# A searched instruction order for an attention and two feed-forward layers: new priorities and an explicit table

## The chip, the cores and the metric

The kernel runs on one core of a Trainium2 chip. The metric is the device time of one execution in microseconds (us). The core has five instruction queues: TensorE (PE, matrix products; PEld is its weight load), VectorE (DVE), ScalarE (ACT), GpSimd (POOL) and SyncE (SP, which issues the DMAs). Each queue runs its instructions strictly in the order of the program, and they wait for one another by semaphores. So the order in which a planner emits the work is the whole schedule.

## The reference

Three stages follow one another: causal attention with a learned decay (4 batches, 8 heads, 576 positions, head size 64), a feed-forward layer 512 → 2048 → 512 with PReLU, and a second one with Mish. Both feed-forward layers see 2304 tokens.

```python
scores = scale * np.matmul(q, k.transpose(0, 1, 3, 2))
cum = np.cumsum(np.log(np.clip(f, 0.0001, 1.0)), axis=-1)
scores = np.where(causal, -1e9, scores + cum[:, :, :, None] - cum[:, :, None, :])
attn = np.exp(scores - np.max(scores, axis=-1, keepdims=True))
attn = attn / (np.sum(attn, axis=-1, keepdims=True) + 1e-09)
x = np.matmul(attn, v)            # then heads side by side: 2304 x 512
h = x @ w_in; g = np.maximum(h, 0.0) + alpha * np.minimum(h, 0.0); x = g @ w_out
h = x @ w_in2; g = h * np.tanh(np.log1p(np.exp(h))); out = g @ w_out2
```

The weights come as 64-bit floats and are turned into 32-bit ones on the core.

## The kernel before

**Stages.** Attention works on 16 pairs of heads. For each pair there are twelve score products that serve only the row maximum (L616, written to one of three PSUM banks b4, b5, b6). VectorE reduces each of them (L623) and so frees its bank. Five small transposes (L635) bring the maxima into rows; then come the scores themselves (L660, banks b0 to b3 in twos), the exponential (L670 on ScalarE), the sums (L708) and the product with v (L742, banks b4 to b6 again). X holds the result, 512 x 2304.

Each feed-forward product is done in three passes: both operands are split into a high part in the reduced 32-bit format and a low part, the rest (L321 casts the high part, L331 subtracts for the low one). For the activations these are xh and xl, for the hidden layer g, for the weights w. L786 to L788 are the first product (three passes, four chunks of 512, 384 tokens to a block, six blocks); below, three such passes are a unit. L851 to L853 are the second product of layer 1, L862 to L864 that of layer 2. In layer 1, four of the sixteen slices of the hidden layer are done first for each block (`group_a`, products on bank b7 during the attention and on b4 to b7 after it; L323 or L321 copies their result out), for three blocks while the attention still runs. The other twelve follow in `moe_block`. Weights arrive as 64-bit words and are converted by L399 (ACT) and L401, L403, L405 (DVE); those of layer 2 are converted during layer 1, stored, and fetched back.

At the start GpSimd and VectorE fill constant tiles (L527 to L553). One of them is the unit matrix `ident` (masks.py:197 and 199). TensorE then runs 30 products of it with itself (L519, "warm", 60 instructions in the trace), and four more behind each of the first pair's products. The decay goes f → clamp (L532) → logarithm (L533, ACT) → running sum (L534) → high part (L537, ACT) and low part (L538), and from there by DMA (L579) into three rows of KM, an operand of L616.

**What sets the order.** Every operation is added to `Plan` with its engine, a cost in us, a wanted time `at` and the things it reads and writes. `PRIO` (by stage name and number in the stage) shifts the wanted time; `ENG` picks the engine where two or three could do the operation. `schedule` is a list scheduler: the engine that is free first takes the ready operation with the smallest priority, with `HOP` for a handover between engines and a rule that GpSimd and some VectorE work exclude each other (`door`). `emit` runs it ten times, forward and backward by turns, keeps the order with the smallest estimate, and calls the operations in that order. PSUM banks of the shared groups are taken from that best schedule (`self.taken`).

Of the kernel before, what the change touches and what calls it, by code (L numbers as in the profile page):

```python
# [16 lines left out]

PRIO = {'': {0: -17.5, 1: -17.2, 2: -11, 3: -11.5, 4: -11.4}, 'A0': {0: -1.0, 1: -1, 2: 7.5, 3: -8.5}, 'A0g': {1: -13.5, 2: -16.5, 3: -21.1}, 'A1': {0: 50, 1: -24.7, 2: 1, 3: -42.4}, 'A1g': {0: -16.6, 1: 5, 2: 6, 3: -0.2}, 'A2': {0: 48.5, 2: -4, 3: 15.2}, 'A2g': {0: 12, 1: -22.0, 2: 30.6, 3: 15}, 'A3': {0: 9.5, 1: -8, 2: -42.3, 3: -28.5}, 'A3g': {0: 31, 1: 4, 2: 54.2, 3: -6}, 'AX': {1: 10.1, 2: 21.5, 3: -5, 4: 12, 5: 11.5, 6: 25.1, 7: 21}, 'B0': {0: 1.3, 1: -1.3, 2: 2, 3: 8, 4: -1}, 'B1': {0: 0.5, 2: -26.9, 3: 2, 4: -17.3}, 'B2': {0: 4.5, 1: 0.5, 2: -31.4, 3: 7.5, 4: 8.5}, 'B3': {0: -15.7, 1: 24, 2: -57.2, 3: 7, 4: 1.5, 5: -3.5, 6: 1.4, 7: 2.5}, 'H0': {0: -1, 1: -0.5, 2: -2.5, 3: -33, 4: 9, 5: 16.5, 6: 11.5, 7: 10}, 'H1': {0: -45.2, 1: -4.5, 2: -40.5, 3: -36.5, 4: -2.5, 5: 4.5, 6: 1, 7: 8, 8: -70.4, 9: -7.1, 10: 3.7, 11: -4, 12: -33.6, 13: -5.5, 14: -30.5}, 'LB2': {0: -1.6, 1: 2, 2: 2, 3: 2}, 'LQ2': {0: -38.9, 1: 20}, 'LV2': {0: 6.3, 1: 20}, 'M2': {0: 20, 1: 6.1, 2: 20, 3: 27.7, 4: 20, 5: 20, 6: 20, 7: -2.4, 8: 20, 9: 21.2, 10: 16.0, 11: 47.1, 12: 20, 13: 30.5, 14: 20, 15: 20, 16: 20, 17: 20, 18: 20, 19: 30.1, 20: 20, 21: 20.5, 22: 20, 23: 20.6}, 'NM2': {0: 0.6, 2: 4.6}, 'O0': {0: -1, 1: -8.5, 2: -11.1, 3: -37, 4: 29.1, 5: 2.5, 6: -0.5, 7: -0.1}, 'O1': {0: -8.5, 1: 22.5, 2: 17.4, 3: 41.2, 4: -9.7, 5: 25, 6: 15.8, 7: 36.5, 8: 62.5}, 'R2': {6: -0.3, 7: -4.9, 9: -1.8, 10: 3.8, 11: -25.5}, 'ST0': {1: 3.2, 3: -4.8}, 'ST1': {0: -6.4, 2: -1.6}, 'ST2': {2: -17.2}, 'ST3': {3: 53.3}, 'T2': {0: -5, 1: -5, 2: -5, 3: -5}, 'W': {0: 36.6, 1: -4, 2: -12.5, 3: -7.6, 4: 34, 5: -33.3, 6: -58.3, 7: 9.5, 8: 30, 9: -6.5, 10: -29.8, 11: -5, 12: 1, 13: -25.9}, 'WA': {0: 2, 1: 4.0, 3: -24.8, 4: -10.5, 5: 6.5, 6: 2, 7: 5, 8: -41.5, 9: -12.9, 10: -6.3, 11: 10.8, 12: 7.5}, 'WF': {0: 33.9, 1: 5.4, 2: -47.5}, 'WS': {0: 1, 1: 4.2, 2: -17, 3: -56, 4: -2, 5: -12.8, 6: -1.4, 7: -6.7, 8: -15.5, 9: -26, 10: -6.8, 11: -40.8, 13: -5.5}, 'X0': {0: -1.6, 1: -52.2, 2: 38.0, 3: -5, 4: -2, 5: 11.5, 6: 22.0, 7: -19.1}, 'X1': {0: -10.8, 1: -14.4, 2: -13.2, 3: -22, 4: -4.5, 5: 16.4, 6: -22.5, 7: -49.3}, 'alph': {0: 60.6, 1: 32.4}, 'const': {0: 46.5, 1: 2}, 'pro2': {1: -42.3, 3: -16.0, 7: -1.2, 8: -7.9, 11: 10.3, 12: 7.7, 13: 19.7, 18: -5.1, 21: -1.9, 22: 17.9, 24: -4.5, 25: 15.7, 26: -9.5, 27: 35.1}, 'warm2': {0: 6.0}}  # L20
ENG = {('A0g', 0): 'ACT', ('A0g', 2): 'ACT', ('A0g', 3): 'POOL', ('A1g', 0): 'ACT', ('A2g', 2): 'ACT', ('A2g', 3): 'DVE', ('A3g', 0): 'DVE', ('AX', 1): 'DVE', ('AX', 2): 'ACT', ('AX', 3): 'DVE', ('AX', 4): 'ACT', ('AX', 5): 'DVE', ('AX', 7): 'DVE', ('B0', 4): 'DVE', ('B3', 4): 'DVE', ('H0', 4): 'ACT', ('H0', 7): 'DVE', ('H1', 13): 'ACT', ('H1', 14): 'DVE', ('NM2', 1): 'ACT', ('NM2', 2): 'ACT', ('O1', 3): 'DVE', ('O1', 5): 'ACT', ('R2', 3): 'POOL', ('T2', 2): 'ACT', ('T2', 3): 'ACT', ('WF', 2): 'DVE', ('X0', 0): 'ACT', ('X0', 1): 'POOL', ('X0', 2): 'ACT', ('X0', 3): 'POOL', ('X0', 4): 'ACT', ('X0', 6): 'ACT', ('X0', 7): 'POOL', ('X1', 0): 'ACT', ('X1', 3): 'POOL', ('X1', 5): 'POOL', ('X1', 6): 'ACT', ('X1', 7): 'POOL'}


class Plan:
# [1017 lines left out]
```

## Time and profile before

| | us |
|---|---|
| median of 3 runs | 1030.71 (1030.51 to 1034.02) |
| the profiled execution, its own time | 1031.08 |
| its span, first to last instruction | 1029.4 |

The profiled execution lies 0.37 us over the median, and 1.68 us of its time lie outside the span. [...] TensorE is busy in 98% of the span. The attention takes up to about 270 us, with three `group_a` blocks in it; layer 1 follows to about 628 us; layer 2 fills the rest.

How to read it: with one engine busy nearly always, the time is what that engine's instructions take plus the gaps between them. A busy TensorE in these profiles includes pipelining, so a gap can also hide in the distance from one start to the next, without being called idle.

### The profile page before, as it was taken

The page shows a single profiled execution, that of the slowest core. Times are in us where ns is not written, and L with a number is a line of the kernel's source. Part 1 is how long each engine was busy: PE and PEld are TensorE (multiplying, and loading weights), DVE is VectorE, ACT ScalarE, POOL GpSimd, SP SyncE. Part 2 cuts the span into 40 slices and gives each one's busy share as a digit, 9 for nine tenths or more (in the row PEclk, how much of TensorE's full clock was granted, in tenths as well). Part 3 has the DMA queues.
Part 4 walks back from the last instruction along what each step waited for, and adds up shares of the span by engine and source line. Part 5 has one row for each costly group of instructions (what it writes and reads, how often), then busy time and mean ns, then how long its engine had stood idle before and what let it go on. Part 6 is the DMA issues. An engine that isn't in the chain of part 4 may idle for free.

```text
span 1029.4 us, 16893 instructions
## 1 busy us (share of the span) xinstructions
PE 1009.9 (98%) x5996; PEld 909.7 (88%) x5996; DVE 746.0 (72%) x1751; ACT 537.7 (52%) x1127; POOL 336.7 (33%) x351
## 2 busy tenths in 40 slices
...
GB/s 167 82 106 106 92 52 57 73 49 13 32 100 115 144 116 203 185 238 170 175 1 1 43 112 114 22 1 32 1 11 21 1 31 1 1 32 1 32 1 31
DMA packets 55397, 71.05 MB, mean 69 GB/s; under 512 B 6672, under 2 KB 32272, under 8 KB 55312
## 3 DMA queue, kind: packets, MB, share of 16 engines
q1 hardware_dynamic: 55312, 69.97, 21.6%
...
## 4 chain that ended last, share of the span: by engine, by line
PE 91%; DVE 5%; issue 1%; POOL 1%; ACT 1%; DMA 0%; DVEq 0%; POOLq 0%; ACTq 0%
PE b L786 13%; PE b L787 12%; PE b L788 12%; PE b L864 6%; PE b L863 6%; PE b L862 6%; PE b L851 6%; PE b L853 6%; PE b L660 6%; PE b L852 6%; PE b L742 4%; PE b L616 3%; PE b L519 2%; PE b L708 2%; DVE junk L623 1%
## 5 line engine op out<-in xcount | busy, mean ns | idle before, releaser
L786 PE MATMUL b<-xh,w 128*128 128x384 f32 x768 | 259.0, 337 | 2.3 <-DVE x L323 2.1
L788 PE MATMUL b<-xl,w 128*128 128x384 f32 x768 | 257.4, 335 | 0.0
L787 PE MATMUL b<-xh,w 128*128 128x384 f32 x768 | 257.3, 335 | 0.0
L843 POOL TENSOR_TENSOR x<-x 128x384 f32<-128x384 f32 x96 | 111.6, 1164 | 249.6 <-DVE x L841 193.2
L786 PEld LDWEIGHTS b<-xh,w 128*128 128x128 f32 x768 | 144.2, 188 | 8.7 <-DVE x L323 3.0
L787 PEld LDWEIGHTS b<-xh,w 128*128 128x128 f32 x768 | 144.3, 188 | 3.3 <-POOL w L331 0.3
L788 PEld LDWEIGHTS b<-xl,w 128*128 128x128 f32 x768 | 144.2, 188 | 0.0
L851 PE MATMUL b<-g,w 128*128 128x384 f32 x384 | 130.3, 339 | 1.4 <-DVE x L814 1.2
L853 PE MATMUL b<-g,w 128*128 128x384 f32 x384 | 128.9, 336 | 0.7 <-POOL g L331 0.3
L852 PE MATMUL b<-g,w 128*128 128x384 f32 x384 | 128.4, 334 | 0.0
L321 ACT CAST g<-x 128x384 fp32r<-128x384 f32 x120 | 61.6, 513 | 107.4 <-POOL x L843 55.0
L864 PE MATMUL b<-w,g 128*128 128x512 f32 x288 | 113.2, 393 | 0.0
L863 PE MATMUL b<-w,g 128*128 128x512 f32 x288 | 113.0, 392 | 0.0
L862 PE MATMUL b<-w,g 128*128 128x512 f32 x288 | 112.8, 392 | 0.0
L623 DVE CUSTOM_DVE_ANT_0 junk<-b,tri 128x320 f32<-128x320 f32 (+3 forms) x160 | 69.4, 434 | 49.7 <-PE b L616 37.9
L331 DVE TENSOR_TENSOR g<-x,g 128x384 fp32r<-128x384 f32 x102 | 71.9, 707 | 38.2 <-ACT g L321 37.6
L811 DVE SCALAR_TENSOR_TENSOR X<-X,alph,b 128x384 f32<-128x384 f32 x72 | 43.8, 611 | 56.8 <-ACT X L805 56.5
L805 ACT ACTIVATE X<-b 128x384 f32<-128x384 f32 x72 | 35.3, 490 | 81.1 <-PE b L788 79.5
L331 POOL TENSOR_TENSOR xl<-X,xh 128x384 fp32r<-128x384 f32 x18 | 19.4, 1087 | 174.1 <-ACT xh L321 126.8
L851 PEld LDWEIGHTS b<-g,w 128*128 128x128 f32 x384 | 72.1, 188 | 4.3 <-DVE x L814 1.8
L670 ACT ACTIVATE Pt<-b 128x288 f32<-128x288 f32 (+1 forms) x128 | 56.4, 502 | 37.2 <-PE b L660 36.7
L853 PEld LDWEIGHTS b<-g,w 128*128 128x128 f32 x384 | 72.1, 188 | 1.9 <-DVE g L331 1.3
...
## 6 DMA issues: line engine op xcount, KB each, us to landing
...
```

The lines of the kernel that those rows point to most:

```text
L331: plan.add(engs, 0.0, at, lambda e: (nc.gpsimd if e == "POOL" else nc.vector).tensor_tensor(out=out(), in0=in0(), in1=in1(), op=ALU.subtra ...
L623: nc.vector.tensor_tensor_reduce(out=junk[ql, :z - a], in0=ps()[ql, :z - a], in1=tri[ql, x0 + a:x0 + z], scale=-1.0, scalar=BIG if n == 0 ...
L786: nc.tensor.matmul(ps[:, :NB], w[:, 0, c], xh[c], start=(c == 0), stop=False)
L787: nc.tensor.matmul(ps[:, :NB], w[:, 1, c], xh[c], start=False, stop=False)
L788: nc.tensor.matmul(ps[:, :NB], w[:, 0, c], xl[c], start=False, stop=(c == KC - 1))
L843: add("POOL", c_pool(NB, 2.2), lambda e, m: nc.gpsimd.tensor_tensor(out=m, in0=e, in1=m, op=ALU.mult), [ek, mk], [mk])
L851: nc.tensor.matmul(ps[:, :NB], w[:, 0, c], g[:, 0], start=first, stop=False)
L852: nc.tensor.matmul(ps[:, :NB], w[:, 1, c], g[:, 0], start=False, stop=False)
L853: nc.tensor.matmul(ps[:, :NB], w[:, 0, c], g[:, 1], start=False, stop=last)
L862: nc.tensor.matmul(ps, g[:, 0, sl], w[:, 0], start=first, stop=False)
L863: nc.tensor.matmul(ps, g[:, 0, sl], w[:, 1], start=False, stop=False)
L864: nc.tensor.matmul(ps, g[:, 1, sl], w[:, 0], start=False, stop=last)
```

## The change

Nothing is computed in another way: the counts of every kind of matmul and of every DMA stay as they are. Three things differ. 164 values of `PRIO` are new or changed. In `ENG`, the low part of the activations of layer 2 (stage X1) moves to VectorE for two more of the four chunks, and that of one chunk in layer 1 (X0); one of the three result copies of layer 2 (O1) moves from VectorE to ScalarE. And `emit` puts the first 3391 of the 5138 operations in the order of a table. The table holds all of the attention and of layer 1, the storing of layer 2's weights and most of their fetching, and the first 77 operations of layer 2 itself. What is left follows in the list schedule's order.

```diff
-ENG = {('A0g', 0): 'ACT', ('A0g', 2): 'ACT', ...
+ENG = {('A0g', 0): 'ACT', ('A0g', 2): 'ACT', ('A0g', 3): 'POOL', ('A1g', 0): 'ACT', ('A2g', 0): 'DVE', ...
+ORDER = [int(x) for x in """
+11 23 12 20 29 15 16 17 24 5 14 13 3 31 27 38 37 32 26 25 34 33 35 21 40 0 56 84 89 85 90 18 10 9 110 52 51
...
+""".split()]
...
         _, order, found, users = best
+        head = set(ORDER)
+        order = ORDER + [n for n in order if n not in head]
         self.taken = {("use", u): b for u, (b, _) in found.items()}
```

In the changed kernel every line number from L321 on is higher by 157 (L519 is L676, L616 is L773, L635 is L792, L786 is L943, L851 is L1008). The texts below use the old ones.

**GpSimd at the start.** These rows stand at the head of GpSimd's queue before; QM, KM, M and BK are operand tiles that get constants.

```order
L548 MEMSET KM_1_135 64x576
L546 MEMSET QM_1_131 64x576
L546 MEMSET QM_1_131 3x576
L528 ISA
L528 AFFINE_SELECT tri<-tri 128x128
L550 MEMSET M_142 128x640
L548 MEMSET KM_1_137 64x576
L549 MEMSET BK_138 128x640
L546 MEMSET QM_1_133 64x576
L546 MEMSET QM_1_133 3x576
masks.py:197 MEMSET ident 128x128
masks.py:199 AFFINE_SELECT ident<-ident 128x128
```

Now `ident` comes right behind one tile:

```order
L703 MEMSET QM_1_131 64x576
L703 MEMSET QM_1_131 3x576
masks.py:197 MEMSET ident 128x128
masks.py:199 ISA
masks.py:199 AFFINE_SELECT ident<-ident 128x128
```

The two instructions that make `ident` moved from behind nine fills and a mask to behind two fills; those passed now follow it.

**TensorE at the end of the first pairs' maxima.** b4 to b6 are the three banks of L616; M51 holds the maxima that the transposes read. Before, six L616 stand in a row:

```order
L660 MATMUL b1_66<-BQ0_140,BK0_138 128x192
L519 MATMUL b7_72<-ident_73 128x128 x4
L616 MATMUL b4_69<-KM1_1_137,QM1_1_133 128x320
L616 MATMUL b5_70<-KM1_0_136,QM1_0_132 128x192
L616 MATMUL b6_71<-KM1_1_137,QM1_1_133 128x192
L616 MATMUL b4_69<-KM0_0_134,QM0_0_130 128x320
L616 MATMUL b5_70<-KM0_1_135,QM0_1_131 128x320
L616 MATMUL b6_71<-KM0_0_134,QM0_0_130 128x256
L635 MATMUL b2_67<-ident_73,M51_143 128x128 x3
L635 MATMUL b3_68<-ident_73,M51_143 128x128 x2
L616 MATMUL b4_69<-KM0_1_135,QM0_1_131 128x256
```

Now four stand there, and the transposes come two rows earlier:

```order
L817 MATMUL b1_66<-BQ0_140,BK0_138 128x192
L676 MATMUL b7_72<-ident_73 128x128 x4
L773 MATMUL b5_70<-KM1_0_136,QM1_0_132 128x192
L773 MATMUL b6_71<-KM1_1_137,QM1_1_133 128x192
L773 MATMUL b4_69<-KM0_0_134,QM0_0_130 128x320
L773 MATMUL b5_70<-KM0_1_135,QM0_1_131 128x320
L792 MATMUL b2_67<-ident_73,M51_143 128x128 x3
L792 MATMUL b3_68<-ident_73,M51_143 128x128 x2
L773 MATMUL b4_69<-KM0_1_135,QM0_1_131 128x256
L773 MATMUL b6_71<-KM0_0_134,QM0_0_130 128x256
L773 MATMUL b5_70<-KM0_0_134,QM0_0_130 128x64
```

One product of the next pair (KM0, QM0; 128x256) went from before the transposes to behind them, and the 128x320 of KM1 that opened the run went up ahead of a score group.

**TensorE behind the attention.** This is the second product of a `group_a` block (g0 to g3) and the first product of the next one (xh, xl), which needs bank b4 copied out. Before, three units stand between the last product on b4 and the next block's first:

```order
L852 MATMUL b4_69<-g3_107,w3_1_87 128x384
L853 MATMUL b4_69<-g3_107,w3_1_87 128x384
L851 MATMUL b5_70<-g1_105,w1_1_83 128x384
L852 MATMUL b5_70<-g1_105,w1_1_83 128x384
L853 MATMUL b5_70<-g1_105,w1_1_83 128x384
L851 MATMUL b6_71<-g1_105,w1_1_83 128x384
L852 MATMUL b6_71<-g1_105,w1_1_83 128x384
L853 MATMUL b6_71<-g1_105,w1_1_83 128x384
L851 MATMUL b6_71<-g2_106,w2_1_85 128x384
L852 MATMUL b6_71<-g2_106,w2_1_85 128x384
L853 MATMUL b6_71<-g2_106,w2_1_85 128x384
L786 MATMUL b4_69<-xh0_96,w0_0_80 128x384
```

Now there are six of them, of which the first four are left out here:

```order
L1008 MATMUL b4_69<-g3_107,w3_1_87 128x384
L1009 MATMUL b4_69<-g3_107,w3_1_87 128x384
L1010 MATMUL b4_69<-g3_107,w3_1_87 128x384
...
L1008 MATMUL b6_71<-g1_105,w1_1_83 128x384
L1009 MATMUL b6_71<-g1_105,w1_1_83 128x384
L1010 MATMUL b6_71<-g1_105,w1_1_83 128x384
L1008 MATMUL b5_70<-g3_107,w3_1_87 128x384
L1009 MATMUL b5_70<-g3_107,w3_1_87 128x384
L1010 MATMUL b5_70<-g3_107,w3_1_87 128x384
L943 MATMUL b4_69<-xh0_96,w0_0_80 128x384
```

Products on b7 and b5 moved up into that stretch, from behind the next block's first product.

## Rows read from the trace of the kernel before

**Rows 1.** The page, part 1: engine, busy us, share of the span, instructions.

```profile
PE 1009.9 (98%) x5996; PEld 909.7 (88%) x5996; DVE 746.0 (72%) x1751; ACT 537.7 (52%) x1127; POOL 336.7 (33%) x351
```

**Rows 2.** Busy us per 50 us stretch, instructions in brackets; clock, DMA share, GB/s last.

```profile
500.00:550.00 50.00, 50.00 (x290) 50.00 (x290) 20.19 (x40) 15.13 (x31) 3.05 (x3) 1.00 0.16 48
700.00:750.00 50.00, 50.00 (x254) 45.30 (x253) 36.98 (x73) 25.58 (x53) 15.98 (x15) 1.00 0.04 17
```

**Rows 3.** Waits of TensorE: waiter, releaser; us in total, times, longest.

```profile
PE b L616 <- DVE M L623: 2.3, 6, 0.6
PE b L786 <- DVE x L323: 2.1, 3, 1.2
```

**Rows 4.** Timeline, all engines, start of the program: start, us, engine, line, operation.

```profile
0.80 0.57 POOL L531 MEMSET Pt<- 32x576 f32 x1 [0.29 <-POOLq L1019]
...
1.82 1.19 POOL L546 MEMSET QM<- 64x576 f32 x2
...
4.34 1.50 DVE L532 TENSOR_SCALAR Pt<-Pt 32x576 f32<-32x576 f32 x1
...
5.88 0.68 ACT L533 ACTIVATE Pt<-Pt 32x576 f32<-32x576 f32 x1 [3.80 <-DVE Pt L532]
...
6.31 0.19 POOL masks.py:197 MEMSET ident<- 128x128 f32 x1
...
6.92 9.24 PE L519 MATMUL b<-ident 128*128 128x128 f32 x60 [6.92 <-POOL ident masks.py:199]
...
7.62 1.35 DVE L534 TENSOR_TENSOR_SCAN Pt<-Pt,tri 32x576 f32<-32x576 f32 x1
...
9.71 0.75 DVE L538 SCALAR_TENSOR_TENSOR Pt<-Pt 32x576 fp32r<-32x576 f32 x1 [0.74 <-ACT Pt L537]
...
10.54 1.63 SPq L579 DMA_DIRECT2D KM<-Pt  x2
...
13.51 0.84 SPq L393 DMA_DIRECT2D raw<-in_moe_w_out_dram  x2
...
15.92 0.39 PE L616 MATMUL b<-KM,QM 128*128 128x320 f32 x1
...
16.26 1.03 ACT L399 ACTIVATE wb<-raw 128x256 f32<-128x256 f32 x2 [2.07 <-DMA raw<-in_moe_w_out_dram]
16.35 0.49 DVE L623 CUSTOM_DVE_ANT_0 junk<-b,tri 128x320 f32<-128x320 f32 x1 [2.74 <-PE b L616]
```

**Rows 5.** Timeline of TensorE, 39 to 43 us, a run of six L616 matmuls.

```profile
39.86 0.59 PE L616 MATMUL b<-KM,QM 128*128 128x320 f32 x3
40.85 1.41 PE L616 MATMUL b<-KM,QM 128*128 128x320 f32 x3 [0.39 <-DVE M L623]
42.10 0.71 PE L635 MATMUL b<-ident,M 128*128 128x128 f32 x5
```

**Rows 6.** Timeline of TensorE, 262 to 267.5 us, around an L742 group.

```profile
263.21 0.34 PE L853 MATMUL b<-g,w 128*128 128x384 f32 x1
263.47 2.92 PE L742 MATMUL b<-Pt,vt 128*64 128x256 f32 x28
266.33 0.44 PE L851 MATMUL b<-g,w 128*128 128x384 f32 x1
266.61 0.34 PE L852 MATMUL b<-g,w 128*128 128x384 f32 x1
266.78 0.34 PE L853 MATMUL b<-g,w 128*128 128x384 f32 x1
```

**Rows 7.** Timeline, all engines, 285 to 287.5 us, after the attention.

```profile
285.13 0.34 PE L853 MATMUL b<-g,w 128*128 128x384 f32 x1
...
286.05 0.54 DVE L323 COPY x<-b 128x384 f32<-128x384 f32 x1
...
286.65 0.44 PE L786 MATMUL b<-xh,w 128*128 128x384 f32 x1 [1.19 <-DVE x L323]
```

**Rows 8.** Groups by line of the low-part subtraction in the second feed-forward layer.

```profile
L331 POOL TENSOR_TENSOR xl<-x,xh 128x384 fp32r<-128x384 f32 x18 | 20.5, 1159 | 64.5 <-DVE xl L331 39.8 <-ACT xh L321 19.1 <-PE b L863 5.6
...
L331 DVE TENSOR_TENSOR xl<-x,xh 128x384 fp32r<-128x384 f32 x6 | 3.4, 564 | 5.5 <-ACT xh L321 5.5
```

More of the change, by code (lines that the diff above doesn't have):

```diff
@@ L16 @@
 PSUM = bass.MemoryType.PSUM
-PRIO = {'': {0: -17.5, 1: -17.2, 2: -11, 3: -11.5, 4: -11.4}, 'A0': {0: -1.0, 1: -1, 2: 7.5, 3: -8.5}, 'A0g': {1: -13.5, 2: -16.5, 3: -21.1}, 'A1': {0: 50, 1: -24.7, 2: 1, 3: -42.4}, 'A1g': {0: -16.6, 1: 5, 2: 6, 3: -0.2}, 'A2': {0: 48.5, 2: -4, 3: 15.2}, 'A2g': {0: 12, 1: -22.0, 2: 30.6, 3: 15}, 'A3': {0: 9.5, 1: -8, 2: -42.3, 3: -28.5}, 'A3g': {0: 31, 1: 4, 2: 54.2, 3: -6}, 'AX': {1: 10.1, 2: 21.5, 3: -5, 4: 12, 5: 11.5, 6: 25.1, 7: 21}, 'B0': {0: 1.3, 1: -1.3, 2: 2, 3: 8, 4: -1}, 'B1': {0: 0.5, 2: -26.9, 3: 2, 4: -17.3}, 'B2': {0: 4.5, 1: 0.5, 2: -31.4, 3: 7.5, 4: 8.5}, 'B3': {0: -15.7, 1: 24, 2: -57.2, 3: 7, 4: 1.5, 5: -3.5, 6: 1.4, 7: 2.5}, 'H0': {0: -1, 1: -0.5, 2: -2.5, 3: -33, 4: 9, 5: 16.5, 6: 11.5, 7: 10}, 'H1': {0: -45.2, 1: -4.5, 2: -40.5, 3: -36.5, 4: -2.5, 5: 4.5, 6: 1, 7: 8, 8: -70.4, 9: -7.1, 10: 3.7, 11: -4, 12: -33.6, 13: -5.5, 14: -30.5}, 'LB2': {0: -1.6, 1: 2, 2: 2, 3: 2}, 'LQ2': {0: -38.9, 1: 20}, 'LV2': {0: 6.3, 1: 20}, 'M2': {0: 20, 1: 6.1, 2: 20, 3: 27.7, 4: 20, 5: 20, 6: 20, 7: -2.4, 8: 20, 9: 21.2, 10: 16.0, 11: 47.1, 12: 20, 13: 30.5, 14: 20, 15: 20, 16: 20, 17: 20, 18: 20, 19: 30.1, 20: 20, 21: 20.5, 22: 20, 23: 20.6}, 'NM2': {0: 0.6, 2: 4.6}, 'O0': {0: -1, 1: -8.5, 2: -11.1, 3: -37, 4: 29.1, 5: 2.5, 6: -0.5, 7: -0.1}, 'O1': {0: -8.5, 1: 22.5, 2: 17.4, 3: 41.2, 4: -9.7, 5: 25, 6: 15.8, 7: 36.5, 8: 62.5}, 'R2': {6: -0.3, 7: -4.9, 9: -1.8, 10: 3.8, 11: -25.5}, 'ST0': {1: 3.2, 3: -4.8}, 'ST1': {0: -6.4, 2: -1.6}, 'ST2': {2: -17.2}, 'ST3': {3: 53.3}, 'T2': {0: -5, 1: -5, 2: -5, 3: -5}, 'W': {0: 36.6, 1: -4, 2: -12.5, 3: -7.6, 4: 34, 5: -33.3, 6: -58.3, 7: 9.5, 8: 30, 9: -6.5, 10: -29.8, 11: -5, 12: 1, 13: -25.9}, 'WA': {0: 2, 1: 4.0, 3: -24.8, 4: -10.5, 5: 6.5, 6: 2, 7: 5, 8: -41.5, 9: -12.9, 10: -6.3, 11: 10.8, 12: 7.5}, 'WF': {0: 33.9, 1: 5.4, 2: -47.5}, 'WS': {0: 1, 1: 4.2, 2: -17, 3: -56, 4: -2, 5: -12.8, 6: -1.4, 7: -6.7, 8: -15.5, 9: -26, 10: -6.8, 11: -40.8, 13: -5.5}, 'X0': {0: -1.6, 1: -52.2, 2: 38.0, 3: -5, 4: -2, 5: 11.5, 6: 22.0, 7: -19.1}, 'X1': {0: -10.8, 1: -14.4, 2: -13.2, 3: -22, 4: -4.5, 5: 16.4, 6: -22.5, 7: -49.3}, 'alph': {0: 60.6, 1: 32.4}, 'const': {0: 46.5, 1: 2}, 'pro2': {1: -42.3, 3: -16.0, 7: -1.2, 8: -7.9, 11: 10.3, 12: 7.7, 13: 19.7, 18: -5.1, 21: -1.9, 22: 17.9, 24: -4.5, 25: 15.7, 26: -9.5, 27: 35.1}, 'warm2': {0: 6.0}}
@@ L21 @@
-ENG = {('A0g', 0): 'ACT', ('A0g', 2): 'ACT', ('A0g', 3): 'POOL', ('A1g', 0): 'ACT', ('A2g', 2): 'ACT', ('A2g', 3): 'DVE', ('A3g', 0): 'DVE', ('AX', 1): 'DVE', ('AX', 2): 'ACT', ('AX', 3): 'DVE', ('AX', 4): 'ACT', ('AX', 5): 'DVE', ('AX', 7): 'DVE', ('B0', 4): 'DVE', ('B3', 4): 'DVE', ('H0', 4): 'ACT', ('H0', 7): 'DVE', ('H1', 13): 'ACT', ('H1', 14): 'DVE', ('NM2', 1): 'ACT', ('NM2', 2): 'ACT', ('O1', 3): 'DVE', ('O1', 5): 'ACT', ('R2', 3): 'POOL', ('T2', 2): 'ACT', ('T2', 3): 'ACT', ('WF', 2): 'DVE', ('X0', 0): 'ACT', ('X0', 1): 'POOL', ('X0', 2): 'ACT', ('X0', 3): 'POOL', ('X0', 4): 'ACT', ('X0', 6): 'ACT', ('X0', 7): 'POOL', ('X1', 0): 'ACT', ('X1', 3): 'POOL', ('X1', 5): 'POOL', ('X1', 6): 'ACT', ('X1', 7): 'POOL'}
+PRIO = {'': {0: -2.5, 1: -9.8, 2: -9, 3: -9.5, 4: -9.4}, 'A0': {0: -1.0, 1: -8.9, 2: 7.9, 3: -8.2}, 'A0g': {0: -13.4, 1: -28.5, 2: -16.5, 3: -71.9}, 'A1': {0: 49.1, 1: -24.7, 2: 1, 3: -42.4}, 'A1g': {0: -16.6, 1: 11.2, 2: 32.9, 3: -0.2}, 'A2': {0: 102.9, 2: -13.4, 3: 11.0}, 'A2g': {0: -6.6, 1: -14.6, 2: 17.1, 3: 11.5}, 'A3': {0: 9.5, 1: -8, 2: -42.3, 3: -28.7}, 'A3g': {0: 31, 1: -0.6, 2: 54.3, 3: -11.0}, 'AX': {0: 1.9, 1: 18.9, 2: 19.4, 3: 6.4, 4: 12, 5: 11.5, 6: 25.1, 7: 22.3}, 'B0': {0: 1.3, 1: -1.3, 2: 2, 3: 8, 4: 1.7}, 'B1': {0: 0.5, 1: -2.4, 2: -28.8, 3: 2, 4: -17.3}, 'B2': {0: 4.5, 1: 0.5, 2: -37.9, 3: 7.5, 4: 6.4}, 'B3': {0: -15.7, 1: 18.2, 2: -57.2, 3: 7, 4: 6.1, 5: -6.1, 6: 1.4, 7: 12.0}, 'H0': {0: -1, 1: -0.5, 2: -2.5, 3: -48.3, 4: 9, 5: 16.5, 6: 11.5, 7: 10}, 'H1': {0: -47.2, 1: -6.5, 2: -42.5, 3: -38.5, 4: 7.7, 5: -12.3, 6: 5.0, 7: 7.9, 8: -120.1, 9: -9.1, 10: 1.7000000000000002, 11: -6, 12: -35.6, 13: -7.5, 14: -25.1}, 'LB2': {0: -6.9, 1: -17.8, 2: -16, 3: -17.7}, 'LQ2': {0: -37.5, 1: 20}, 'LV2': {0: -10.4, 1: 20}, 'M2': {0: 20, 1: 19.3, 2: 20, 3: 22.0, 4: 20, 5: 21.6, 6: 20, 7: -2.4, 8: 20, 9: 21.2, 10: 16.0, 11: 47.1, 12: 20, 13: 30.5, 14: 20, 15: 20, 16: 20, 17: 20, 18: 20, 19: 30.1, 20: 20, 21: 18.7, 22: 20, 23: 24.9}, 'NM2': {0: 0.6, 1: -0.1, 2: 4.5}, 'O0': {0: 1, 1: -6.5, 2: -9.1, 3: -35, 4: 28.8, 5: 3.4, 6: 0.6000000000000001, 7: 25.5}, 'O1': {0: -8.5, 1: 22.5, 2: 17.4, 3: 43.1, 4: -28.7, 5: 15.7, 6: 15.8, 7: 36.5, 8: 62.5}, 'R2': {0: 13.0, 2: -10.6, 3: -1.8, 5: 4.2, 6: -0.3, 7: 2.0, 9: -1.8, 10: 3.8, 11: -25.5}, 'ST0': {0: -0.5, 1: -9.4, 2: -0.5, 3: -6.6}, 'ST1': {0: -6.4, 2: -2.8}, 'ST2': {1: 2.0, 2: 0.3, 4: 43.4}, 'ST3': {2: 7.2, 3: 53.2, 4: -21.4}, 'T2': {0: -3.6, 1: -2, 2: -2, 3: -4.4}, 'V2': {2: -2.2}, 'W': {0: 26.6, 1: -4, 2: -12.5, 3: -7.6, 4: 38.5, 5: -33.3, 6: -58.9, 7: 9.5, 8: 30, 9: -6.5, 10: -22.5, 11: -5, 12: 1, 13: -25.9}, 'WA': {0: 2, 1: 4.0, 3: -24.8, 4: -9.6, 5: 6.5, 6: 2.3, 7: 5, 8: -41.5, 9: -12.9, 10: -10.4, 11: 10.8, 12: 7.5, 13: 22.8}, 'WF': {0: 33.9, 1: 6.7, 2: -47.5}, 'WS': {0: -5.4, 1: 2.2, 2: -17, 3: -58, 4: -4, 5: -16.8, 6: -12.6, 7: -7.9, 8: -15.5, 9: -30.2, 10: 19.2, 11: -42.8, 12: -27.8, 13: -38.2}, 'X0': {0: -1.9, 1: -53.6, 2: 38.0, 3: -5, 4: -2, 5: 11.5, 6: 22.0, 7: -19.1}, 'X1': {0: -48.4, 1: -54.4, 2: -52.3, 3: -58.8, 4: -53.6, 5: -8.2, 6: -62.5, 7: -97.2}, 'alph': {0: 60.6, 1: 71.1}, 'const': {0: 51.5, 1: 7}, 'pro2': {0: 19.2, 1: 1.5, 2: 10, 3: -6.0, 4: 10, 5: 10, 6: 6.4, 7: 8.8, 8: 2.0999999999999996, 9: 10, 10: 10.6, 11: 20.3, 12: 17.7, 13: 48.8, 14: 23.9, 15: 10, 16: 41.8, 17: 10, 18: 4.9, 19: -24.7, 20: 4.7, 21: 8.1, 22: 27.9, 23: 9.8, 24: 5.5, 25: 25.9, 26: 0.5, 27: 42.1, 28: 64.0}, 'warm2': {0: -19.0}}
```

1 line of the change is left out of this document (added), and 149 rows, old and new, of the table ORDER.

## Prediction

> **What bounds the kernel.** The page comes first: TensorE is busy 98% of the span, the next engine 72% [rows 1]. So the time is TensorE's own work and the gaps in it. The stretches of 50 us come second. In layer 1 and layer 2 TensorE is busy for 50.00 of 50 us, and VectorE, which feeds it, for 20 and 37 [rows 2]. No order of instructions can shorten these stretches; it can only break them. What can be won lies in the first 300 us: the start, the waits inside the attention, and the step from attention to layer 1. The list of waits names only 2.3 us for the maximum products (L616) and 2.1 us for the first products of a block [rows 3]. These are idle times alone. More is hidden in the distance from start to start: six L616 in a row take 2.24 us from the first to the transposes (42.10 - 39.86), where the first three need 0.59 [rows 5]. Two times 0.59 is 1.18, so 1.06 us are waiting there, of which 0.39 is called idle.
>
> All instructions on TensorE are as many as before, so each term below is a gap that opens or closes. The sum is made against the profiled execution, 1031.08 us.
>
> **The start: -3.7.** TensorE's first instruction waits for `ident` until 6.92, since GpSimd begins it only at 6.31, 0.61 before TensorE's start [rows 4]. In the new order two fills of QM stand ahead of it, 1.19 us together, and the first fill begins at 0.80. So TensorE starts at 0.80 + 1.19 + 0.61 = 2.60, which is 4.3 earlier. The 30 warm products take 15.92 - 6.92 = 9.00 us, hence the first L616 can't come before 11.60. It did not wait before, TensorE ran straight into it; now its operand KM could be late. KM waits for the chain of the decay. The clamp began at 4.34; in the new order one fill of KM fewer and three very short ones more stand ahead of it, and I leave it there. The logarithm ended at 5.88 + 0.68 = 6.56, but the running sum began only at 7.62, behind fills. These are gone from that place, so the sum runs from 6.56 to 7.91, the low part (L538) keeps its 0.74 us of waiting for ScalarE and ends at 7.91 + 0.74 + 0.75 = 9.40, where it ended at 10.46 before. The DMA of KM follows 0.08 later, at 9.48. No row tells when it lands. The nearest one is the 256 KB load that is issued at 13.51 and lets ScalarE go at 16.26, 2.75 us later [rows 4]; 6.8 KB should take no longer. So KM is there by 12.2, and the warm products bound it from below with 11.6. The first L616 comes 3.7 to 4.3 us earlier than at 15.92. If the chain of the decay gained nothing it would be 10.54 + 2.75 = 13.3, a gain of 2.6. A fill of QM that now stands behind L538 on VectorE comes due at about the same time. I take 3.7, the value for the later landing, and keep 2.6 and 4.3.
>
> What stands behind it on the queues moves along. The fills that `ident` overtook are of KM and the other operands. GpSimd does them while the warm products run: some ten of about 0.57 us [rows 4] end by 8.6, before the DMA of KM.
>
> **Maximum products: -3.5.** A bank of L616 is free when VectorE has reduced it: the product starts at 15.92, the reduction at 16.35 and takes 0.49, so 0.92 after the start, and TensorE goes on 0.06 after such an end (286.05 + 0.54 against 286.65) [rows 4, 7]. Less 0.1 for the product itself, some 0.9 us of other TensorE work must stand between two uses of a bank. I went through both orders and put TensorE's shortest distances of the trace on the rows between. Before, 23 of 162 such re-uses have less than 0.9 us between them, and what is missing adds up to 7.3 us; now 11 of 163, and 2.8 us. That is 4.5. From the run of six, with three re-uses for 1.06 us, it is 0.35 each, and 12 fewer are 4.2. The second row group shown of the orders is one such place: two re-uses in the run where there were three. Bounds: 0, if VectorE is late for other reasons and the waits only change their place, and -7.3, if none is left. I take -3.5, a little under the two prices, since the reductions also queue behind conversions on VectorE.
>
> **Transposes: +0.6.** They need the last reduction of their pair, and the product that it reads is nearer now: 8 of 16 stand less than 0.9 us behind it, 3 before. What is missing to 1.0 us is 2.0 us instead of 1.4.
>
> **Changes of tile form: +1.8.** L660 works on 64x128 tiles of the array, L708 and L742 on 128x64, all else on 128x128. Going into such a group and out of it costs: from 263.21 to 263.47 are 0.26 us, and from 266.33 to 266.61 are 0.28, where 0.17 lies between two products (266.61 to 266.78) [rows 6]. So 0.09 and 0.11. Between the first transposes and the last product with v the order changes form 129 times before and 147 times now: 18 x 0.10 = 1.8. It can be 0 where TensorE would have waited anyway. [...]
>
> **Behind the attention: -1.2.** The first product of the next block waited 1.19 us for the copy of bank b4, which ended at 286.59 [rows 7]. Six units of 0.52 us (three times 0.17) now stand before it instead of three, 1.56 us more, and ahead of that copy VectorE has two subtractions fewer than before. The wait goes. What may be late next is the second product of the block after it, which waits for the same VectorE; bounds -1.2 and +1.2.
>
> **The low parts on VectorE: 0.** In layer 2, 12 subtractions go from GpSimd (1159 ns each) to VectorE (564 ns) [rows 8]. At a block's start that is 1.7 us on VectorE and 1.2 on GpSimd, where there were 0.6 and 3.5. TensorE has second products of the block before to do meanwhile, which is why no wait shows there now. VectorE gets 6.8 us more in 400 us, at 37 of 50 busy. The result copies moved to ScalarE: 0, since the last one stood there before.
>
> The sum: -3.7 - 3.5 + 0.6 + 1.8 - 1.2 = -6.0, so 1025.1 us for an execution like the profiled one. That lay 0.37 over the median of the runs, so I predict 1024.7.
>
> **The rivals.**
> - The waits only move. [...] For it: seven of the sixteen transposes now stand at 0.78 to 0.85 us, just short of what VectorE needs, as if the order had been packed to a limit that the chip does not quite hold. Against it: VectorE has 28% of its time free [rows 1]. A start that gains nothing, because KM or the fill of QM comes late, ends near it: -6.0 + 3.7 = -2.3, 1028.4. Together 0.26.
> - [...] 0.15.
> - Slower: the subtractions on VectorE are the place. If each of the 6 blocks of layer 2 starts with 1.7 us of waiting behind the Mish work on VectorE, and each of the 6 of layer 1 with 0.56, that is 13.6 us: 1024.7 + 13.6 = 1038.3. It turns the result to slower than before from 6.0 / 12 = 0.5 us per block start on. For it: these stretches have no gap at all, so any wait counts in full. Against it: VectorE has 13 of 50 us free there, and GpSimd's part, which it replaces, took twice as long. 0.09.
>
> **Chances and range.** The forecast has 0.50, with 1021.5 to 1027.5 as its own range. Half a per cent, about what a measurement of this kernel can tell from no change, is 5.2 us: faster means under 1025.6. Two thirds of the forecast lie there, 0.33, with the second rival 0.48; I say 0.50, since the two prices of the banks were both higher than my value. Slower: 0.09. The same: 0.41. The range 1018.5 to 1031.0 leaves out the deepest part of the second rival and the third.
>
> **What would show it.** The start of L519 near 2.6 us and the first L616 (now L773) between 11.6 and 12.3; a later one means that KM or QM was late. Six L616 in a row gone, and the idle time of TensorE before the maxima under 1 us in the list of waits. No idle TensorE of over 1 us between 270 and 300. TensorE busy 50.00 of 50 us from 350 on; a lower figure there, with VectorE's L331 (now L488) as the releaser, is the third rival, and would make the prediction wrong.

## The result and the profile after

The changed kernel takes 1020.29 us (median of 4 runs, 1018.46 to 1022.9) against 1030.61 us for the kernel before on the same chip: a ratio of 0.9894, 95% interval 0.9875 to 0.9914. By the ratio that is 10.9 us, by the two medians 10.3, where 6.0 were forecast. The profiled execution is the slowest of the four: 1022.9 us, span 1021.2. A second profile of the same program (experiment e5) has a span of 1018.4; where the two differ, both are given. One execution of all those reported here, the profiled one of e4 (1238.79 us at a mean granted clock of 0.753), was in a slower state of the chip and is in no comparison.

In the profile after, lines are higher by 157. The page's part 1, answering to [rows 1]:

```profile
PE 1007.9 (99%) x5996; PEld 910.4 (89%) x5996; DVE 737.4 (72%) x1763; ACT 538.5 (53%) x1133; POOL 314.8 (31%) x333
```

The two stretches of [rows 2], and the one ahead of the first, same columns:

```profile
450.00:500.00 50.00, 48.65 (x281) 48.36 (x280) 32.66 (x79) 17.57 (x44) 2.33 (x2) 1.00 0.36 121
500.00:550.00 50.00, 49.30 (x285) 48.98 (x284) 30.18 (x76) 17.62 (x44) 2.03 (x2) 1.00 0.32 101
700.00:750.00 50.00, 50.00 (x254) 45.41 (x253) 40.41 (x76) 26.54 (x54) 14.58 (x13) 1.00 0.01 1
```

In the two stretches of [rows 2] VectorE has more to do (30 and 40 us of 50, where it had 20 and 37), over the whole span less (737.4 us against 746.0). TensorE is busy 50.00 of 50 us in the stretch of layer 2. In layer 1 it lacks 0.70 us from 500 to 550, where it had 50.00, and 1.35 from 450 to 500, where it had 49.90. TensorE's waits, which answer to [rows 3] (waiter, releaser; us in total, times, longest):

```profile
PE b L676 <- POOL ident masks.py:199: 2.6, 1, 2.6
PE b L773 <- DMA KM<-Pt: 2.1, 1, 2.1
PE b L943 <- DVE X L968: 1.3, 1, 1.3
PE b L773 <- DVE M L780: 1.0, 2, 0.8
PE b L1010 <- DVE g L488: 0.7, 1, 0.7
PE b L945 <- DVE xl L488: 0.5, 1, 0.5
PE b L943 <- DVE x L480: 0.5, 1, 0.5
```

The wait of the maximum products (L773, formerly L616) for VectorE fell from 2.3 us in six places to 1.0 in two (I had named under 1), and that of the first products for the copy L480 from 2.1 to 0.5. A row of before that I had not counted is gone too:

```profile
PE b L851 <- DVE x L814: 1.2, 1, 1.2
```

New is the second row of the list after: the first maximum product waits 2.1 us for KM, which comes by DMA. The start, answering to [rows 4] (timeline, all engines):

```profile
0.80 1.20 POOL L703 MEMSET QM<- 64x576 f32 x2 [0.29 <-POOLq L1176]
...
2.56 9.42 PE L676 MATMUL b<-ident 128*128 128x128 f32 x60 [2.56 <-POOL ident masks.py:199]
...
3.21 1.19 POOL L703 MEMSET QM<- 64x576 f32 x2
...
3.95 4.28 DVE L689 TENSOR_SCALAR Pt<-Pt 32x576 f32<-32x576 f32 x1
...
4.36 0.62 POOL L707 MEMSET M<- 128x640 f32 x1
4.93 0.23 POOL L710 MEMSET kt<- 128x64 f32 x2
5.11 0.57 POOL L705 MEMSET KM<- 64x576 f32 x1
5.63 0.62 POOL L706 MEMSET BK<- 128x640 f32 x1
6.20 0.57 POOL L705 MEMSET KM<- 64x576 f32 x1
6.72 0.62 POOL L707 MEMSET M<- 128x640 f32 x1
7.29 0.62 POOL L706 MEMSET BK<- 128x640 f32 x1
7.97 0.40 POOL L708 MEMSET vt<- 64x128 f32 x1
...
8.97 1.34 DVE L691 TENSOR_TENSOR_SCAN Pt<-Pt,tri 32x576 f32<-32x576 f32 x1 [0.75 <-ACT Pt L690]
...
11.08 0.74 DVE L695 SCALAR_TENSOR_TENSOR Pt<-Pt 32x576 fp32r<-32x576 f32 x1
...
11.91 1.58 SPq L736 DMA_DIRECT2D KM<-Pt  x2
...
14.07 0.39 PE L773 MATMUL b<-KM,QM 128*128 128x320 f32 x1 [2.09 <-DMA KM<-Pt]
14.30 1.66 PE L676 MATMUL b<-ident 128*128 128x128 f32 x8
```

TensorE starts at 2.56, as forecast. But the clamp on VectorE (L689) takes 4.28 us, where it took 1.50, and the chain behind it moves the DMA of KM to 11.91, later than the 10.54 of before. The first maximum product comes at 14.07: 1.85 earlier than before, not 3.7. Then TensorE's granted clock falls to 0.50, in this execution. The same one in windows (TensorE's busy time behind the length of the window; granted clock, 1.00 in full, third from the end):

```profile
14.00:14.57 0.57, 0.49 (x4) 0.53 (x5) 0.39 (x2) 0.43 (x2) 0.00 (x0) 1.00 0.04 12
14.57:17.98 3.41, 3.41 (x18) 3.41 (x18) 1.51 (x5) 0.88 (x2) 1.56 (x3) 0.50 0.85 250
17.98:20.00 2.02, 2.02 (x20) 2.02 (x20) 1.52 (x7) 1.09 (x2) 0.00 (x0) 1.00 0.27 104
```

For 3.41 us the granted clock is 0.50, half of the 1.00 ahead of it and behind it. The eight products of `ident` at 14.30 take 1.66 us; in the kernel before the like of them (16.15, granted clock 1.00) take 1.05. The first transposes start at 28.30, before at 28.80: of the 4.36 us won at TensorE's start 0.50 are left.

The run of six maximum products [rows 5] is now one of four:

```profile
39.10 0.62 PE L773 MATMUL b<-KM,QM 128*128 128x192 f32 x3
39.90 0.42 PE L773 MATMUL b<-KM,QM 128*128 128x320 f32 x1 [0.18 <-DVE M L780]
40.15 0.91 PE L792 MATMUL b<-ident,M 128*128 128x128 f32 x5
```

From its first product to the transposes are 1.05 us, before 2.24. And the first product behind the attention that waits for a copy, answering to [rows 7]:

```profile
296.84 0.44 PE L943 MATMUL b<-xh,w 128*128 128x384 f32 x1 [0.50 <-DVE x L480]
```

It waits 0.50 us, before 1.19. Between 270 and 300 us no wait of TensorE is longer than 0.54.

**Where the time went.** TensorE's first 2300 instructions are the same set in both orders (by line and count), so the distances from each start to the next one can be added up by line; a wait counts with the instruction before it. Old line numbers, us, before against the two profiles of the changed kernel:

| TensorE instructions, first 2300 | before | after | e5 | after less before | forecast |
|---|---|---|---|---|---|
| start of the first L519 | 6.92 | 2.56 | 2.56 | -4.36 | |
| L519, 188 | 22.92 | 26.55 | 26.27 | +3.63 | start: -3.7 |
| L616 maxima, 192 | 46.30 | 40.45 | 40.42 | -5.85 | -3.5 |
| L635 transposes, 80 | 8.46 | 8.73 | 8.73 | +0.27 | +0.6 |
| L660, L708, L742, 1216 | 129.30 | 130.79 | 130.79 | +1.49 | +1.8 |
| L786 to L788 first products, 336 | 61.83 | 62.07 | 62.09 | +0.25 | |
| L851 to L853 second products, 288 | 57.94 | 52.92 | 52.63 | -5.02 | -1.2 |

The column adds up to -9.6 us at the 2300th instruction. At the span's end it is -8.2 in this profile (1.4 is given back in the layers) and -11.0 in e5 (0.8 more is won there).

### The profile page after: what moved, and what is told of

Same layout as the page of the kernel before. It is cut to its first block, busy times and chain, and to the rows that moved or that the text cites. A ratio compares the mean times of both kernels' runs of the same rounds, so it can differ in the third digit from the quotient of the medians.

```text
span 1021.2 us, 16756 instructions
## 1 busy us (share of the span) xinstructions
PE 1007.9 (99%) x5996; PEld 910.4 (89%) x5996; DVE 737.4 (72%) x1763; ACT 538.5 (53%) x1133; POOL 314.8 (31%) x333
## 4 chain that ended last, share of the span: by engine, by line
PE 89%; DVE 5%; DMA 2%; ACT 1%; issue 1%; POOL 0%; SPq 0%; DVEq 0%; ACTq 0%
PE b L943 12%; PE b L945 12%; PE b L944 12%; PE b L1021 7%; PE b L1020 6%; PE b L1019 6%; PE b L817 6%; PE b L1008 6%; PE b L1010 5%; PE b L1009 5%; PE b L899 4%; PE b L773 3%; PE b L676 2%; PE b L865 2%; DMA raw<-in_moe_w_out_dram 1%
## 5 line engine op out<-in xcount | busy, mean ns | idle before, releaser
L943 PE MATMUL b<-xh,w 128*128 128x384 f32 x768 | 259.0, 337 | 2.0 <-DVE X L968 1.3
L943 PEld LDWEIGHTS b<-xh,w 128*128 128x128 f32 x768 | 144.2, 188 | 7.4 <-issue 2.5
L1008 PE MATMUL b<-g,w 128*128 128x384 f32 x384 | 129.6, 337 | 0.0
L1010 PE MATMUL b<-g,w 128*128 128x384 f32 x384 | 128.6, 335 | 0.7 <-DVE g L488 0.7
L488 DVE TENSOR_TENSOR g<-x,g 128x384 fp32r<-128x384 f32 x102 | 69.3, 681 | 38.0 <-ACT g L478 37.2
L556 ACT ACTIVATE wb<-raw 128x256 f32<-128x256 f32 x128 | 52.0, 431 | 82.0 <-DMA wd<-wb 32.9
L994 DVE SCALAR_TENSOR_TENSOR b<-x 128x384 f32<-128x384 f32 x96 | 63.4, 661 | 14.4 <-ACT x L993 13.4
L1008 PEld LDWEIGHTS b<-g,w 128*128 128x128 f32 x384 | 72.1, 188 | 1.7 <-issue 1.5
L1010 PEld LDWEIGHTS b<-g,w 128*128 128x128 f32 x384 | 72.1, 188 | 1.0 <-DVE g L488 1.0
L1009 PEld LDWEIGHTS b<-g,w 128*128 128x128 f32 x384 | 72.1, 188 | 0.0
```

Of the source, the lines that this page charges most:

```text
L488: plan.add(engs, 0.0, at, lambda e: (nc.gpsimd if e == "POOL" else nc.vector).tensor_tensor(out=out(), in0=in0(), in1=in1(), op=ALU.subtra ...
L943: nc.tensor.matmul(ps[:, :NB], w[:, 0, c], xh[c], start=(c == 0), stop=False)
L1008: nc.tensor.matmul(ps[:, :NB], w[:, 0, c], g[:, 0], start=first, stop=False)
L1009: nc.tensor.matmul(ps[:, :NB], w[:, 1, c], g[:, 0], start=False, stop=False)
L1010: nc.tensor.matmul(ps[:, :NB], w[:, 0, c], g[:, 1], start=False, stop=last)
```

## The experiments

Each kernel was timed beside the kernel before on the same chip; a ratio is to that one, and the us won are worked out from the ratio (the medians of e1 to e3 differ by 7.2, 2.6 and 2.4). Where an edit is a reordered table, the fence tells it in words.

**e1: the new order up to the end of the attention alone.**

```diff
-order = the changed kernel's
+order = its first 1488 operations, then the others as in the kernel before (with that kernel's ENG for the two layers)
```

> The first 1488 operations in the order of the changed kernel (all of the attention, the start included), the rest in the order of before; engines by the same split. Theory 1 (the gain is made up to the last product with v): TensorE's 2000th instruction and the last L742 come as early as in the changed kernel, 2.3 to 7 us before those of the kernel before, and the time is 1022 to 1025 us. Rival (the gain is made behind the attention and in the feed-forward layers, the shorter bank waits are lost again there): 1028 to 1031 us.

Measured 1024.08 us (1023.38 to 1025.04) against 1031.27, ratio 0.9926 (0.9912 to 0.9941): about 7.6 us. The wait for KM (2.4 us) is there, and so are the waits that stand behind the attention (L851 for L814 1.2, L786 for L323 1.2). By line, maxima -5.86, second products -1.62.

**e2: the reverse, only what stands behind the attention.**

> The attention in the order of before, all behind it in the order of the changed kernel. Theory 1: the wait for bank b4 behind the attention goes, 1 to 3 us by 292 us, and about 2 us are given back in the layers, as in the changed kernel's trace: 1028.5 to 1031 us. Rival: 1021 to 1025 us.

Measured 1028.67 us (1027.78 to 1030.23), ratio 0.9971 (0.9959 to 0.9982): about 3.0 us, with the maxima unchanged (+0.21) and the second products -2.52. The two parts, 7.6 and 3.0, make up the whole. The step behind the attention is worth more than the 1.2 forecast.

**e3: the new priorities and engines without the table.**

```diff
-        order = ORDER + [n for n in order if n not in head]
```

> The new priorities and engines, without the table: the list schedule's own order. ident stands late on GpSimd's queue again. Theory 1 (the table makes the gain, by the early start and the spread of L616): TensorE starts near 6.9 us and the time is 1026 to 1031 us. Rival (the priorities make it, the table is a trimming of under 2 us): 1020 to 1024 us.

Measured 1028.87 us (1026.91 to 1029.87), ratio 0.9967 (0.9955 to 0.998). So the list schedule with the new numbers gives 3.4 us, and the table the other 7 or so. TensorE starts at 6.95 here: the early `ident` is the table's doing.

**e5, e6, e7: the changed kernel once more, with `ident` late, and with 42 warm products.**

```diff
 e6: on GpSimd, ident moved back behind a mask and nine more fills
 e7:
-    WARM = 30
+    WARM = 42
```

> The changed kernel once more, as the measure for the three beside it: 1019 to 1022 us, with the granted clock at half for 3.41 us in the runs whose mean clock is 0.998.

> The changed kernel with ident moved back behind nine fills of GpSimd. TensorE starts near 7 us, the warm products reach to about 16, no wait for KM and no half clock. Theory 1 (in the changed kernel the early start gains 1.9 us until the first L616, and the half clock takes 1.7 of it): 0 to 1.5 us slower than the changed kernel. Rival (the start is worth 3.7 us, as in my sum): 3 to 4 us slower.

> The changed kernel with 42 warm products instead of 30, so that TensorE has work until KM lands. Theory 1 (the wait of 2.1 us for KM lets the clock fall to half, and that costs 1.7 us): the warm products end near 14.1, no half clock, 1 to 2 us faster than the changed kernel. Rival (the half clock is hidden behind VectorE's reductions there): the same within 0.5 us.

Against 1031.83 us for before: e5 1019.9 (ratio 0.988, 0.9864 to 0.9897), e6 1021.53 (0.99, 0.9885 to 0.9916), e7 1018.84 (0.9873, 0.9855 to 0.989).

e6 starts TensorE at 7.22, 4.66 later, and is only 1.6 us slower than e5. That is not the price of the late start alone: its clamp takes 2.71 us, the DMA of KM is issued at 10.38 instead of 11.91, TensorE runs into the first maximum product (16.35) without a wait, and the clock does not fall (mean granted clock 1.000). At the first transposes (28.96) it is 0.92 behind e5.

In e7 the warm products reach to the landing of KM. There is no wait and the granted clock stays at 1.00. The first maximum product comes 0.38 us later than in e5 (14.46, 14.08) and the first transposes nevertheless 0.96 earlier (27.08, 28.04). By the two medians the half clock costs about 1.1 us (1019.9 - 1018.84), though the intervals of the two overlap. The nine runs of the changed kernel, the four above and the five of e5, point the same way. Four of them have a mean granted clock of 1.000 and took 1018.46 to 1019.79 us; five have 0.998, as 3.41 us at a clock of 0.50 make it, and took 1019.9 to 1022.9. So the clock fell in a part of the executions only.

**e8: the changed kernel with one pair of fills moved.** Two fills of QM, the pair at 3.21 above, go behind three others in GpSimd's queue.

```diff
 GpSimd: Pt, tri mask,
-  QM 64x576, QM 3x576, M, kt, kt, KM, BK, ...
+  M, kt, kt, QM 64x576, QM 3x576, KM, BK, ...
```

> The changed kernel with one pair of GpSimd's fills (QM of the second product, 64x576 and 3x576) moved behind three others (M, kt, kt). Theory (the clamp of f, 4.28 us on VectorE instead of 1.50, is held up by GpSimd's fills that follow each other without a break, and a pair of fills of one tile has a break in it): the clamp ends near 5.6 instead of 8.23, KM's DMA is issued near 9.5, the first L616 starts at 11.7 to 12.3, and the time is 2.5 to 4 us under the changed kernel's. Rival (the clamp waits for something else, the load of f for one): it takes over 4 us again, and the time is the same.

Measured 1017.38 us (1016.34 to 1018.16), ratio 0.9858 (0.984 to 0.9875). This beats both kernels, the changed one by 2.5 us (e5, timed beside it). Timeline of its start:

```profile
3.94 0.89 DVE L532 TENSOR_SCALAR Pt<-Pt 32x576 f32<-32x576 f32 x1
3.95 1.40 POOL L546 MEMSET QM<- 64x576 f32 x2
...
5.58 1.35 DVE L534 TENSOR_TENSOR_SCAN Pt<-Pt,tri 32x576 f32<-32x576 f32 x1 [0.75 <-ACT Pt L533]
...
8.84 0.74 DVE L538 SCALAR_TENSOR_TENSOR Pt<-Pt 32x576 fp32r<-32x576 f32 x1
...
9.67 1.59 SPq L579 DMA_DIRECT2D KM<-Pt  x2
...
11.96 0.39 PE L616 MATMUL b<-KM,QM 128*128 128x320 f32 x1
```

The clamp takes 0.89 us instead of 4.28, KM is there when the warm products end, and the first maximum product comes at 11.96. That is inside the 11.6 to 12.2 of the forecast, but in part by luck. The clamp ends at 4.83, 1.0 earlier than the 5.84 that I had left in place. In return 4.03 us pass from the end of the logarithm (5.55) to that of the low part (9.58), where my sum had 2.84, because conversions of weights stand ahead of it on VectorE, the first of them lengthened:

```profile
6.86 1.41 DVE L401 TENSOR_SCALAR wb<-wb 128x256 int32<-128x256 int32 x1
```

The like of it takes 0.28 at 8.64, when GpSimd's fills are over: the clamp is not the only instruction that is lengthened beside them.

**e4 and e10: the kernel before, with two fills of QM and `ident` at the head of GpSimd's queue.** Both are one program. e4 gave 1029.46 us (median of 11 runs), ratio 0.9978 (0.9967 to 0.9989); the start is read from the profile of e10.

> The kernel before, with nothing moved but the two fills of QM and ident to the head of GpSimd's queue. Theory 1 (an early start counts only as far as KM follows it): TensorE starts at 2.6; KM's DMA is issued near 10.5 as before and lands some 2.2 us later, so the first L616 starts at 12.7 to 13.2 instead of 15.9, and the time is 1027 to 1028 us, or 1029 to 1030 where the clock falls to half in the wait for KM. Rival (my first sum: the start is worth 3.7 us): 1026.9. Second rival (the waits further on swallow it): 1030.6.

> The kernel before, with only the two fills of QM and the unit matrix put at the head of GpSimd's queue, once more, to read its start in a profile. If the clamp on VectorE is held up by GpSimd's unbroken fills, it takes over 2.5 us here too, where it took 1.50; the first L616 comes at 13 to 14.5 us against 15.92. If the clamp does not depend on the fills, it takes 1.5 us and the first L616 comes by 12.2. Time: 1027.5 to 1030 us in either case, since what is won at the start is partly lost again in front of the first transposes.

e10 took 1029.59 us (1028.93 to 1031.19), ratio 0.9986 (0.9977 to 0.9995). By the two ratios the early start alone is worth 1.4 to 2.3 us. At the first transposes (25.99) e10 is 2.81 us ahead of the kernel before, at the 2300th instruction 2.00. For a start in which the clock stays up, as it does here (granted clock 1.00 in every window from 2.60 to 24 us), I had expected 1027 to 1028 us in e4; that was missed. The clamp of e10:

```profile
4.34 1.94 DVE L532 TENSOR_SCALAR Pt<-Pt 32x576 f32<-32x576 f32 x1
...
5.40 1.40 POOL L546 MEMSET QM<- 64x576 f32 x2
...
10.98 1.64 SPq L579 DMA_DIRECT2D KM<-Pt  x2
...
13.12 0.38 PE L616 MATMUL b<-KM,QM 128*128 128x320 f32 x1 [0.72 <-DMA KM<-Pt]
```

The clamp missed what I expected: 1.94 us, not over 2.5, though fills stand around it all the time. So fills as such are not what makes it long.

What fits is a fill behind which GpSimd pauses. The pair of fills of one QM tile has such a pause, of 0.06 us, since its second waits for the first. In five kernels this pair comes while the clamp is on, and each time the clamp ends 0.88 us after the pair's start, by the rows to 0.01, which is 0.31 after the end of its first fill: before 4.96 and 5.84 (4.34 + 1.50), e3 4.99 and 5.87, e2 4.97 and 5.86, e10 5.40 and 6.28, e8 3.95 and 4.83. In the changed kernel the pause in the pair at 3.21 is past before the clamp starts at 3.95, and the fills from 4.36 to 7.91 each begin before the one ahead has ended. The next pause is the one ahead of 7.97 above; the clamp ends at 8.23, again 0.31 (0.32 by the rounded rows) after the end of a fill. e6 fits only in part:

```profile
3.95 2.71 DVE L532 TENSOR_SCALAR Pt<-Pt 32x576 f32<-32x576 f32 x1
...
5.78 0.57 POOL L548 MEMSET KM<- 64x576 f32 x1
6.30 0.50 POOL masks.py:197 MEMSET ident<- 128x128 f32 x1
6.87 0.29 POOL masks.py:199 TENSOR_SCALAR_AFFINE_SELECT ident<-ident 128x128 f32<-128x128 f32 x1
```

The clamp ends at 6.66, 0.31 after the end of the fill of KM, but by the rows there is no pause: the first instruction of `ident` begins at 6.30, 0.05 before that end, and takes 0.50 us instead of 0.19. Why the clamp ended there, and behind none of the eight fills that ended before it in the changed kernel, stays open. Shown is that the order of the fills sets the clamp's time (e8 moves nothing else and has 0.89 us against 4.28); nothing here shows the cause inside the chip.

**e9: the changed kernel with the low parts of the activations back on GpSimd.**

```diff
-ENG X0 1, X1 3, X1 5: DVE
+ENG X0 1, X1 3, X1 5: POOL
```

> The changed kernel with the low parts of the activations back where they were before the change: one chunk in layer 1 and two of layer 2 on GpSimd instead of VectorE, 18 subtractions in all; the order is kept. Prediction's term (moving them is worth 0): 1019 to 1021 us, TensorE busy 50 of 50 us in the blocks of layers 1 and 2. Third rival turned round (work on VectorE at a block's start costs): faster by 1 us or more, below 1018.5. The opposite (GpSimd's 1.16 us at a block's start is what the move took away): slower by 2 us or more, with waits of L786 to L788 for L331 on GpSimd in the list.

Measured 1020.48 us (1019.0 to 1022.22), ratio 0.9893 (0.9878 to 0.9908); e5 had 0.988 (0.9864 to 0.9897). No difference can be told. Its windows in the two layers:

```profile
500.00:550.00 50.00, 50.00 (x291) 50.00 (x290) 31.23 (x75) 18.87 (x46) 4.16 (x4) 1.00 0.35 109
700.00:750.00 50.00, 50.00 (x252) 45.13 (x251) 40.54 (x75) 26.11 (x54) 16.90 (x15) 1.00 0.00 1
```

Its profile also holds a surprise at the start. The wait for KM and the clock behind it:

```profile
PE b L616 <- DMA KM<-Pt: 3.1, 1, 3.1
```

```profile
14.00:15.00 1.00, 0.90 (x8) 0.93 (x9) 0.82 (x2) 0.86 (x2) 0.00 (x0) 1.00 0.11 40
15.00:18.00 3.00, 3.00 (x29) 3.00 (x28) 2.20 (x11) 0.64 (x3) 1.57 (x3) 1.00 0.92 268
```

TensorE waited longer here than in the changed kernel, 3.1 us against 2.1, and kept a granted clock of 1.00. KM came at the same time (14.10, 14.07); the wait is longer because the warm products were over sooner, after 8.46 us where they took 9.42. The first transposes start at 26.71, 1.33 before e5's.

## Why the prediction was right, and where it was not

The direction held, and so did the mechanisms in the attention and behind it. The 6.0 us were too small because two gains were sized too low, by 2.3 and 3.8 us, which is more than the start fell short, 3.0. The errors have opposite signs, and it is partly luck that the total misses by no more than 4 to 5 us.

- **The start, -3.7: wrong, -0.7.** TensorE's start at 2.60 was right (2.56), and the sign that I had named, a first L616 after 12.3, pointed to KM. The step that failed is "I leave it there", said of the clamp. I took its 1.50 us as its own duration. The clamp's time goes with the order of GpSimd's fills: 0.89 us in e8, where a QM fill with a pause behind it starts with the clamp (3.95 and 3.94), and 4.28 in the changed kernel. So the DMA of KM was issued at 11.91 and not at 9.48, and even the rival of a chain that gains nothing (10.54) was too early. Behind the clamp the sum held: 2.88 us from the end of the logarithm (8.94) to that of the low part (11.82), where I had 2.84. The time from issue to use was 2.16 us (14.07 - 11.91), less than the 2.75 I took. In five of nine executions (mean granted clock 0.998) the half clock came with the wait, a second price that the forecast did not have. e8, with the clamp at 0.89 us, has all of the forecast (by the two differences told there): the first maximum product 3.96 earlier than before, and 4.2 at the first transposes (24.58 against 28.80).
- **Maximum products, -3.5: right in kind, too small.** They are 5.85 us less in the profile and in e1 alike, and 6.20 to 6.25 less in e6, e8 and e9, where the clock did not fall (mean granted clock 1.000, 1.000 and 0.999). By the 12 short re-uses that went, this is 0.49 us each, more than the 0.35 of the run of six. The discount for reductions that queue behind conversions had no ground in a row. That the gain is that of the re-uses rests on the count and on the waits that went; no run changes their spacing alone. The rival by which the bank waits only move is out.
- **Transposes, +0.6, and changes of form, +1.8: right**, with +0.27 and +1.49.
- **Behind the attention, -1.2: right in kind, too small.** The 1.19 us [rows 7] went down to 0.50 (the row at 296.84), so the term itself was sized too high. But it was not the only wait there. I priced one wait of several that the list of before held; that of L851 for L814 (1.2 us) and another of L786 are gone with it. e2, which has only this part of the change, gives 3.0 us. In the sums by line the second products have -5.02, of which e1 has -1.62 and e2 -2.52; for the rest of some 0.9 I have no row.
- **Low parts on VectorE, 0: right.** e9 undoes it and moves nothing that can be measured. The third rival, 13.6 us slower, did not come: TensorE is at 50.00 of 50 from 700 to 750. The sign that I had named for it did show in layer 1, by its letter: the 0.70 us missing from 500 to 550 are a wait for VectorE's L488 (L1010 for L488, 0.7). But this is the low part of g, not of the activations that the change moved, and e5 has no such wait. From 450 to 500, where 1.35 are missing, a first product waits 1.35 us for L968 (formerly L811), a step of PReLU on VectorE that reads its bank. Ahead of that step two conversions of weights take 1.12 and 1.23 us beside GpSimd's subtractions, where others of them take 0.41 to 0.43. All seven profiles with the new order behind the attention have one or two waits of this kind, 0.3 to 1.3 us in all; the profiles before, of e1 and of e10 have none. It is a price of the new order that the forecast lacked.
- **Of the rivals**, "the waits only move" (the start, the transposes and the changes of form alone, 1029.4 us) is out. "A start that gains nothing" was true of the start and not of the total. The time lies beneath the forecast's own 1021.5 and nearest to the second rival (all short re-uses, all waits for block starts and the whole start, with the changes of form at 0: 1017.6 us), but not in its way: that rival needed the whole start, and it was the attention and the step behind it that gave more.

The layers gave back 1.4 us in one profile of the changed kernel and won 0.8 in the other. Of these 2.2 us, 1.6 lie in the waits of TensorE behind the 2300th instruction: 2.0 (1.3 and 0.7, above) against 0.4 in e5. Why they differ from run to run of one program stays open.
